# State reads with the token weights held in the array, in a fused attention and MoE kernel

## The chip, the cores and the metric

One core of one Trainium2 chip. The metric is the device time of one execution in microseconds (us), the median of several runs.

## The reference

Each of 8 batches has 8 heads; a head has 512 tokens (x) and 32 states, both 64 wide. Tokens read from states, states read from tokens, and both results, with the heads side by side, go through an MLP with a leaky activation.

```python
scores  = x @ state.T / 8                       # 512 x 32 for each batch and head
a       = softmax(scores, over the states);  xread = a @ state
scores2 = state @ x.T / 8                       # 32 x 512
a2      = softmax(scores2, over the tokens); sread = a2 @ x
rows    = concat([xread, sread]), heads side by side   # 8 * (512 + 32) rows of 512
h       = rows @ w_in                           # 512 x 2048
g       = max(h, 0) + alpha * min(h, 0)
out     = g @ w_out                             # 2048 x 512, float32
```

## The kernel before

The work is cut into small named steps, and one long string, ORDER, lists them in the order in which they are recorded; each engine runs its own steps in that order. So an order that was worked out ahead of time, not a loop, decides what stands behind what. A step is written as name.batch.further numbers; the last number of a step that writes PSUM is its bank.

The steps, by engine:

- GpSimd (POOL): `lx` loads a batch's x, `wi` and `wo` a quarter of w_in and w_out, `lst` the states, all by casting DMAs from float32 to float16; `ssh` subtracts the maximum of each state block, `snorm` divides by the sums, and `tn` (two for a batch, L413) multiplies the token weights by one over their sums.
- TensorE (PE): `xt` transposes x for the first two batches, `sc` computes scores (states as weights, 64x32 tiles), `m` multiplies the states of a head by their rows of w_in (64x32 tiles; h of a token is then its weights over the 8 x 32 states times this product, and xread itself is never computed), `f` and `F` compute h for one block of 128 hidden columns, `S` adds two such blocks to the output of 128 tokens, `L` does so in column pieces for the last tokens of batch 7, `rd` computes the state reads, and `F.8` with `R` takes the 256 state rows through the MLP. `Z` multiplies zeros, at the start alone.
- ScalarE (ACT): `sexp` and `te` (exponentials), `N` (the negative part of h), and most of the copies out of PSUM, `mo` and `O`.
- VectorE (DVE): `sb`, `smax`, `ssum`, `wb` (state softmax on transposed blocks), `tm` and `tsum` (maximum, and one over the sum, of the token softmax), `G` (the activation), and some of the copies.
- SyncE (SP): `xd` and `tt` are transposing DMAs, of x (batches 2 to 7) and of the token weights e2; `O` sends its output rows from here.

What the change touches: `state_reads` (L422) holds x (128 tokens x 64) as weights and streams 32 columns of the transposed token weights; the result has the layout that `XS` needs, so `rdo` only copies it. The token weights were divided by their sums before, by `tn`, ahead of `tt`. Heads 0 to 3 form half 0 and heads 4 to 7 half 1, and within a half the place of head h is `(h - 4 * g) ^ g`. PSUM has six single banks (`single`) and one pair (`two`), which scores use, and some of the m steps. The scores of batch 0 are computed in two halves and a third time as a whole. Tiles for m (7 batches), neg (4), gt and osb (4) come from rotating pools. `O` copies and stores in one step.

Of the kernel before, what the change touches and what calls it, by code (L numbers as in the profile page):

```python
# [8 lines left out]
F32 = mybir.dt.float32  # L9
F16 = mybir.dt.float16  # L10
# [19 lines left out]
G.0.8 G.0.11 N.0.10 S.0.2.3 mo.0.3.a.1 ssh.p.1 S.0.3.0.3 G.0.10 m.1.3 sexp.1 m.2.1.1.2 S.0.0.4  # L30
mo.2.1.a.1 S.0.2.4 mo.2.1.a.0 F.0.14.2 F.0.13.1 ssum.1 N.0.14 S.0.1.4 snorm.p.1 S.0.2.5 G.0.14
S.0.1.5 F.0.15.2 N.0.13 tsum.1 G.0.13 S.0.0.5 F.0.12.1 mo.1.3.a.1 N.0.15 S.0.3.1 S.0.3.2 wb.1 N.0.12
S.0.3.3 G.0.12 S.0.3.4 F.1.2.1 G.0.15 N.1.2 S.0.1.6 mo.1.3.a.0 tn.1.0 G.1.2 S.0.2.6 S.0.1.7 sc.2
tt.0 m.4.2.2.1 S.0.2.7 O.0.1.a F.1.3.0 mo.4.2.a.1 F.1.0.1 mo.4.2.a.0 F.1.1.2 O.0.2.a S.0.0.6 tm.2
N.1.3 N.1.1 S.0.3.5 F.1.5.4 sb.2 tn.1.1 N.1.0 S.0.0.7 G.1.3 lx.3 F.1.7.0 G.1.1 te.2.1 S.0.3.6 N.1.5
G.1.0 N.1.7 te.2.0 F.1.9.2 O.0.0.a G.1.5 N.1.9 S.0.3.7 G.1.7 O.0.3.a tsum.2 F.1.4.1 smax.2 N.1.4
F.1.6.4 S.1.2.0.0 F.1.8.5 G.1.9 tt.1 m.2.3 S.1.2.1 N.1.6 N.1.8 G.1.4 F.1.12.3 G.1.6 F.1.11.2 ssh.p.2
F.1.10.1 S.1.2.2 F.1.15.4 G.1.8 N.1.12 N.1.11 mo.2.3.a.0 S.1.1.0.5 S.1.1.1 N.1.10 S.1.2.3 G.1.12
G.1.11 G.1.10 sexp.2 xd.3 F.1.13.3 N.1.15 S.1.1.2 N.1.13 ssum.2 F.1.14.2 N.1.14 mo.2.3.a.1 S.1.1.3
G.1.13 G.1.14 S.1.2.4 S.1.1.4 S.1.1.5 G.1.15 m.3.2 mo.3.2.a.0 mo.3.2.a.1 m.3.1.1.3 rd.0.2 rd.1.4  # L40
sc.3 snorm.p.2 lx.4 rdo.0.a mo.3.1.v.0 wb.2 rdo.1.a m.2.2.1.2 mo.3.1.v.1 S.1.1.6 xd.4 S.1.2.5
S.1.2.6 F.2.4.4 S.1.1.7 F.2.2.3 mo.2.2.a.1 sb.3 S.1.2.7 S.1.0.0.2 tm.3 mo.2.2.a.0 N.2.4 F.2.15.1
O.1.1.a S.1.0.1 smax.3 S.1.0.2 F.2.0.5 O.1.2.v F.2.9.0 N.2.15 S.1.0.3 G.2.15 ssh.p.3 S.1.0.4 S.1.0.5
N.2.0 N.2.9 tn.2.1 sexp.3 S.1.3.0.1 G.2.0 F.2.13.5 G.2.4 G.2.9 S.1.0.6 te.3.1 ssum.3 N.2.2 N.2.13
G.2.13 F.2.12.4 F.2.8.0 N.2.12 N.2.8 S.1.3.1 S.1.3.2 G.2.12 S.1.3.3 te.3.0 G.2.2 F.2.1.5 S.1.0.7
F.2.5.4 N.2.1 F.2.3.3 G.2.8 S.1.3.4 snorm.p.3 F.2.11.0 tn.2.0 G.2.1 O.1.0.a N.2.5 S.1.3.5 N.2.11
tsum.3 S.1.3.6 N.2.3 G.2.5 m.3.3.2.5 sc.4 wb.3 F.2.6.4 tt.2 G.2.11 mo.3.3.a.1 mo.3.3.a.0 S.1.3.7
S.2.1.0.5 G.2.3 F.3.1.2 N.2.6 F.3.13.0 O.1.3.a F.2.10.3 N.3.1 G.2.6 tm.4 F.2.7.1 N.3.13 N.2.7 N.2.10
te.4.1 S.2.0.0.4 S.2.1.1 G.3.1 S.2.0.1 G.2.7 S.2.0.2 G.2.10 tn.3.1 F.2.14.2 F.3.2.1 N.2.14 S.2.1.2
S.2.1.3 sb.4 G.2.14 N.3.2 F.3.4.3 smax.4 S.2.1.4 S.2.1.5 lx.5 S.2.1.6 N.3.4 G.3.2 S.2.1.7 F.3.14.2  # L50
tn.3.0 O.2.1.a G.3.13 S.2.0.3 F.3.6.1 S.2.3.0.5 te.4.0 ssh.p.4 N.3.14 G.3.14 sexp.4 tsum.4 tn.4.1
N.3.6 G.3.4 S.2.0.4 F.3.8.0 tt.3 N.3.8 S.2.0.5 S.2.3.1 S.2.0.6 S.2.3.2 F.3.3.2 F.3.9.3 ssum.4
snorm.p.4 S.2.3.3 S.2.0.7 N.3.3 xd.5 S.2.3.4 G.3.8 N.3.9 G.3.3 S.2.3.5 m.6.0 G.3.6 G.3.9 m.5.1.0.2
rd.3.1 rd.2.3 O.2.0.a mo.6.0.v.1 mo.5.1.a.0 m.4.1.4.0 mo.5.1.a.1 mo.6.0.v.0 sc.5 rdo.3.a m.4.3.2.1
mo.4.1.a.1 S.2.3.6 F.3.11.0 rdo.2.a mo.4.3.a.0 wb.4 N.3.11 mo.4.1.a.0 S.2.2.0.3 F.3.0.2 mo.4.3.v.1
F.3.10.1 S.2.3.7 tm.5 S.2.2.1 S.2.2.2 G.3.11 N.3.0 F.4.1.4 sb.5 F.3.5.0 S.2.2.3 N.3.10 N.4.1 O.2.3.a
N.3.5 S.2.2.4 G.3.10 G.3.0 F.3.7.1 F.4.11.5 F.4.7.2 lx.6 G.4.1 N.4.11 N.3.7 S.2.2.5 S.2.2.6 smax.5
te.5.0 N.4.7 S.3.3.0.4 lx.7 S.2.2.7 G.3.5 ssh.p.5 S.3.3.1 O.2.2.a te.5.1 S.3.3.2 G.4.7 F.4.5.0
# [11 lines left out]
N.4.12 S.4.1.3 N.5.2 S.4.1.4 G.4.12 S.4.0.4 S.4.1.5 S.4.1.6 F.5.10.1 mo.7.0.a.1 S.4.0.5 ssh.p.6  # L70
G.5.1 sexp.6 G.5.2 F.5.0.5 F.5.5.0 N.5.0 S.4.1.7 S.4.0.6 N.5.10 S.4.0.7 G.5.12 G.5.0 tt.5 S.4.2.0.2
G.5.10 O.4.1.a N.5.5 rd.4.5 O.4.0.v rd.5.3 m.7.3.1.4 G.5.5 rdo.4.a m.6.2.5.0 rdo.5.a mo.6.2.a.0
ssum.6 sc.7 tsum.6 S.4.2.1 snorm.p.6 tn.6.0 S.4.3.0.3 mo.7.3.a.0 S.4.3.1 mo.7.3.v.1 S.4.2.2 F.5.11.5
S.4.3.2 sb.7 S.4.3.3 N.5.11 tn.6.1 G.5.11 F.5.6.1 F.5.9.4 S.4.2.3 S.4.2.4 F.5.7.5 S.4.3.4 mo.6.2.a.1
F.5.8.0 smax.7 S.4.3.5 S.4.3.6 wb.6 S.4.3.7 S.4.2.5 N.5.9 N.5.8 N.5.7 G.5.9 O.4.3.a G.5.8 F.5.4.4
# [12 lines left out]
N.8.2 N.7.2 S.6.2.1 G.8.2 S.6.2.2 N.7.6 S.6.1.7 F.7.14.4 G.7.6 F.7.10.0 G.7.2 S.6.2.3 N.8.9 N.7.14
# [16 lines left out]
def kernel(  # L105
# [51 lines left out]
    xgs = {}  # L157
# [494 lines left out]
```

## Time and profile before

| | |
|---|---|
| time, median of 3 runs | 217.57 us (217.44 to 217.98) |
| profiled execution, first to last instruction | 216.3 us (its own time is not listed apart from this) |
| PE busy | 208.6 us, 1637 matmuls |
| DVE / ACT / POOL busy | 164.8 / 137.6 / 71.1 us |
| HBM read and written | 17.31 and 8.91 MB |

A line of the profile's fifth part names the source line, the engine, the operation, what it writes and reads, shapes and the number of instructions, then busy time, mean nanoseconds of one, and the idle time in front of them with what ended it. In the timeline and in the chain, the first two numbers are the start and the length in us. Matmuls are pipelined: the length of a group holds the last one's way through the array, so the distance between the starts says what one costs.

### The profile page before, as it was taken

What the parts mean: (1) busy time and instruction counts of PE and PEld (TensorE: products, weight loads), DVE (VectorE), ACT (ScalarE), POOL (GpSimd) and SP (SyncE); (2) the same over time, 40 slices, a digit from 0 to 9 for tenths busy, and PEclk for the clock granted to TensorE, in tenths of its full rate; (3) what the DMA queues carried; (4) which work ended last, traced back from release to release, by engine and by line L of the source; (5) the groups of instructions that cost most, each with busy time, mean ns of one, the idle gap of its engine ahead of it and who ended that gap; (6) DMA issues with size and microseconds to landing.
All of it is one profiled execution on the core that took longest, in us unless ns stands there. A gap on an engine that the chain in (4) does not pass through costs nothing.

```text
span 216.3 us, 4190 instructions
## 1 busy us (share of the span) xinstructions
PE 208.6 (96%) x1637; PEld 99.3 (46%) x1637; DVE 164.8 (76%) x253; ACT 137.6 (64%) x271; POOL 71.1 (33%) x58
## 2 busy tenths in 40 slices
PE   7689999999999999999999999999999999999994
PEld 2433334444544444544444445444454455554553
DVE  3699988799999998999886869876798466665001
ACT  3399995998768957879449865566545346544021
POOL 7373858232367626314620112903500000000000
PEclk9999999999999999999999999999999999999999
DMA  6999999888475849596032532031430011110124
GB/s 82 165 202 203 205 187 184 107 240 141 47 129 167 109 88 194 100 192 149 18 83 97 134 63 100 2 97 50 52 147 27 25 48 48 48 48 4 48 100 145
DMA packets 39716, 23.12 MB, mean 107 GB/s; under 512 B 22144, under 2 KB 35984, under 8 KB 39696
## 3 DMA queue, kind: packets, MB, share of 16 engines
q0 software_dynamic: 12704, 8.62, 28.6%
q1 hardware_dynamic: 26960, 14.23, 25.4%
q8 instruction: 13, 0.21, 0.4%
q14 instruction: 7, 0.06, 0.1%
q10 hardware_dynamic: 32, 0.01, 0.0%
HBM read 17.31 MB, written 8.91 MB: 121 GB/s over the span
## 4 chain that ended last, share of the span: by engine, by line
PE 90%; DMA 5%; POOL 2%; issue 1%; ACT 0%; POOLq 0%
PE o L542 50%; PE h L490 25%; DMA w_in_sb<-in_moe_w_in_dram 5%; PE m_ps L457 4%; PE h L499 3%; PE o L590 3%; PE sr_ps L432 2%; PE o L562 2%; PE sc L307 1%; POOL xg L178 1%; POOL xg L161 0%; PE h L511 0%; POOL w_in_sb L197 0%; POOL st L191 0%; POOL ident masks.py:199 0%
## 5 line engine op out<-in xcount | busy, mean ns | idle before, releaser
L542 PE MATMUL o<-w_out_sb,gt 128*128 128x512 f16 x496 | 125.4, 379 | 0.0
L522 ACT ACTIVATE neg<-h 128x512 f32<-128x512 f32 (+1 forms) x144 | 77.6, 582 | 44.5 <-PE h L490 36.3
L530 DVE SCALAR_TENSOR_TENSOR gt<-neg,oma_sb,h 128x512 f16<-128x512 f32 x128 | 89.4, 737 | 18.7 <-ACT neg L522 18.3
L542 PEld LDWEIGHTS <-gt 128*128 128x128 f16 x496 | 47.5, 98 | 54.9 <-issue 2.9
L490 PE MATMUL h<-aT,m 128*128 128x512 f16 x250 | 68.7, 379 | 0.0
L490 PEld LDWEIGHTS <-m 128*128 128x128 f16 x250 | 24.1, 98 | 28.7 <-issue 0.9
L479 ACT CAST m<-m_ps 128x512 f16<-128x512 f32 x49 | 27.0, 603 | 6.4 <-PE m_ps L457 6.0
L413 POOL TENSOR_SCALAR e<-e,r 128x512 f16<-128x512 f16 x16 | 24.9, 1565 | 15.0 <-DVE r L409 13.8
L354 POOL TENSOR_TENSOR ts<-ts,mx 128x1024 f32<-128x1024 f32 (+1 forms) x9 | 15.5, 1719 | 42.2 <-DVE mx L348 42.2
L368 POOL TENSOR_TENSOR an<-ts,r 128x1024 f16<-128x1024 f32 (+1 forms) x9 | 15.4, 1720 | 25.2 <-DVE r L365 16.6
L580 ACT COPY osb<-o 128x512 f32<-128x512 f32 x23 | 13.7, 595 | 14.7 <-PE o L542 14.6
L457 PE MATMUL m_ps<-w_in_sb,stT 64*32 64x512 f16 x256 | 11.3, 383 | 0.5 <-DMA w_in_sb<-in_moe_w_in_dram 0.5
L399 ACT ACTIVATE e<-sc,nb 128x512 f16<-128x512 f32 x16 | 11.1, 704 | 0.4 <-DVE nb L391 0.4
L479 DVE CAST m<-m_ps 128x512 f16<-128x512 f32 x15 | 9.9, 677 | 1.4 <-PE m_ps L457 1.3
L530 DVE SCALAR_TENSOR_TENSOR gs<-neg,oma_sb,h 128x256 f16<-128x256 f32 x16 | 7.5, 476 | 4.5 <-ACT neg L522 4.5
L388 DVE TENSOR_REDUCE nb<-sc 128x2 f32<-128x1024 f32 x8 | 9.7, 1212 | 1.2 <-PE sc L307 1.2
L376 DVE STREAM_TRANSPOSE aT<-an 128x1024 f16<-128x1024 f16 (+1 forms) x9 | 10.0, 1115 | 0.7 <-POOL an L368 0.7
L364 DVE TENSOR_REDUCE r<-ts 128x32 f32<-128x1024 f32 (+1 forms) x9 | 9.8, 1089 | 0.7 <-ACT ts L360 0.7
L348 DVE TENSOR_REDUCE mx<-ts 128x32 f32<-128x1024 f32 (+1 forms) x9 | 9.8, 1090 | 0.0
L499 PE MATMUL h<-XS,w_in_sb 128*128 128x256 f16 x64 | 9.4, 273 | 0.0
L600 DVE COPY osr<-o 128x512 f32<-128x512 f32 x1 | 0.7, 692 | 11.3 <-PE o L590 11.3
L360 ACT ACTIVATE ts<-ts 128x1024 f32<-128x1024 f32 (+1 forms) x9 | 8.7, 971 | 0.0
(52 smaller groups left out, 117.6 us busy)
## 6 DMA issues: line engine op xcount, KB each, us to landing
out_dram<-osb SPq DMA_DIRECT2D x27, 256.0 KB, 2.4
xg<-in_x_dram POOLq DMA_DIRECT2D x7, 512.0 KB, 7.2
w_in_sb<-in_moe_w_in_dram POOLq DMA_DIRECT2D x4, 512.0 KB, 9.0
w_out_sb<-in_moe_w_out_dram POOLq DMA_DIRECT2D x4, 512.0 KB, 8.0
out_dram<-osb SPq DMA_DIRECT2D x9, 128.0 KB, 2.0
xg<-in_x_dram POOLq DMA_DIRECT2D x2, 256.0 KB, 4.9
out_dram<-osr SPq DMA_DIRECT2D x2, 256.0 KB, 2.5
st<-in_state_dram POOLq DMA_DIRECT2D x1, 224.0 KB, 5.6
```

The source lines that it names most:

```text
L354: engine(e).tensor_tensor(ts, ts, over_blocks(cols(live["mx", b], j, S // N)), ALU.subtract)
L368: engine(e).tensor_tensor(blocks(cols(live["an", b], j, S)), blocks(cols(live["ts", b], j, S)), over_blocks(cols(live["r1", b], j, S // N) ...
L399: nc.scalar.activation(live["e2", b][:, g, :, :], live["sc", b][:, :, :, g, :].rearrange("p r j s -> p (r j) s"), EXP, bias=live["nb", b][ ...
L413: nc.gpsimd.tensor_scalar_mul(e2, e2, live["r2", b][:, g : g + 1])
L457: nc.tensor.matmul(t[N * k : N * (k + 1), :], st_head(b, h)[64 * r : 64 * r + 64, :], w_in_sb[64 * r : 64 * r + 64, c, 512 * f : 512 * (f ...
L479: copier(e)(m_tile(b)[:, f, g, :], live["mp", b, f][g])
L490: nc.tensor.matmul(h.rearrange("p (r j s) -> p r j s", r=2, j=2), ms[b][:, f, g, 128 * j : 128 * (j + 1)], weights(b, g), start=(g == 0), ...
L499: nc.tensor.matmul(h, w_in_sb[:, c, 128 * jc : 128 * (jc + 1)], XS[:, c].rearrange("p q n b -> p (q n b)"), start=(c == 0), stop=(c == n_c ...
L522: nc.scalar.activation(neg, h, RELU, bias=0.0, scale=-1.0)
L530: nc.vector.scalar_tensor_tensor(gt, negs.pop((b, jc)), oma_sb[:, jc : jc + 1], h, ALU.mult, ALU.add)
L542: nc.tensor.matmul(outs[b, q], gts[b, jc][:, 128 * q : 128 * (q + 1)], w_out_sb[:, jc, :], start=(jc == 0), stop=(jc == n_jc - 1),)
L580: copier(e)(osb, t)
```

## The change

- `state_reads` swaps its operands: the transposed token weights of a head (128 tokens x 32 states) are the weights, on 128x32 tiles, and x is streamed, 64 columns. Four heads of a half run side by side; the result has states on partitions.
- `tn` is gone. The sums divide the small result: new step `rn` (VectorE, 128x128) multiplies by one over the sum and casts, new step `rt` transposes on TensorE, and `rdo` copies into `XS`.
- Heads of a half are every second one (g, g+2, ...), in loads, transposes, scores and m.
- One tile holds all eight PSUM banks, and every step names its banks; m, neg, gt and osb are fixed places, with the place as one more number of the step.
- `O` only copies; a new step `st` (`Ls` for the pieces) sends the rows, at a place of its own in the order. `S.8` takes the place of `R`.
- Batch 0's scores are computed once, in two halves.
- ORDER is new from end to end.

```diff
     def state_reads(b, bk):
         e2T = live.pop(("e2T", b))
-        t = live["sr", b] = single(bk, f"sr_ps{b}", [128, n_c, N], F32)
-        for c in range(n_c):
-            g = c // 2
+        t = live["sr", b] = single(bk, 2 * D).rearrange("p (g d) -> p g d", g=2)
+        for g in range(2):
             for q in range(n_q):
                 r, j = divmod(q, 2)
-                for i in range(2):
-                    h = 2 * c + i
-                    k = (h - 4 * g) ^ g
+                for k in range(4):
                     nc.tensor.matmul(
-                        t[D * i : D * (i + 1), c, :],
-                        xgs[b][:, h, j, r, :],
+                        t[N * k : N * (k + 1), g, :],
                         e2T[:, g, q, N * k : N * (k + 1)],
+                        xgs[b][:, 2 * k + g, j, r, :],
                         start=(q == 0), stop=(q == n_q - 1),
-                        tile_position=(0, D * i),
+                        tile_position=(0, N * k),
...
+    def state_reads_norm(b):
+        sn = live["sn", b] = att.tile([128, 2, D], F16, name=f"sn_{b}", tag="sn", bufs=2)
+        nc.vector.tensor_tensor(sn, live.pop(("sr", b)),
+            live["r2", b].unsqueeze(2).to_broadcast([128, 2, D]), ALU.mult)
+
+    def state_reads_transposed(b, bk):
+        t = live["srT", b] = single16(bk, 128)
+        nc.tensor.transpose(t, live.pop(("sn", b)).rearrange("p g d -> p (g d)"), ident)
...
-    def token_norm(b, g):
-        e2 = live["e2", b][:, g, :, :]
-        nc.gpsimd.tensor_scalar_mul(e2, e2, live["r2", b][:, g : g + 1])
...
-    def single(k, name, shape, dtype):
-        return ps.tile(shape, dtype, name=name, tag=f"k{k}", bufs=1)
-    def two(name, shape, dtype):
-        return ps.tile(shape, dtype, name=name, tag="two", bufs=1)
+    banks = ps.tile([128, 8, 512], F32, name="ps")
+    def single(k, w=512):
+        return banks[:, k, :w]
+    def two(k0, k1):
+        return banks[:, k0 : k1 + 1, :]
```

The new order where the prediction walks through it, from the loads to the first S steps, and at the end:

```
lx0.0 stc oma lx0.1 lst id wi.0 lx.1 wi.1 wi.2 Z.3.14 ... sc.0.0.6.7 ... wo.0 ssh.p.0.0 ... sc.0.1 ...
m.2.0.1.4 ... m.0.0.2.5 m.3.0.3.0 ... m.1.0.2.5 tt.0 ... wo.1 m.4.0.6.7 ... f.0.0.0.1 f.0.1.0.0 ... f.0.1.1
f.0.2.0.2 ... f.0.2.1 ... m.0.1.6.3 ... f.0.0.1 ... F.0.3.7 ... F.0.7.4 F.0.6.3 ... m.0.2.5.6 ... F.0.4.0 ...
F.0.5.2 ... m.1.1.1.6 ... F.0.10.5 ... F.0.9.4 ... S.0.0.0.7
...
S.8.0.7 L.7.3.0.2 O.8.0.a.2 L.7.3.0.3 L.7.3.0.4 L.7.3.0.5 st.8.0 L.7.3.0.6 L.7.3.0.7 LO.7.3.0.a Ls.7.3.0
```

The old order at the first of these places is `m.2.0 f.0.0.0.5 f.0.1.0.4 wi.2 ... f.0.1.1 ... m.0.1.1.3 f.0.0.1 ... m.1.1`, with `wo.0` ahead of `wi.2`, and it ends in `L.7.3.2.6 L.7.3.2.7 O.7.1.a LO.7.3.2.a`.

More of the change, by code (lines that the diff above doesn't have):

```diff
@@ L41 @@
[L41 to L46, printed above, removed]
@@ L70 @@
[L70 to L75, printed above, removed]
@@ L478, in state_w_in_out, with state_w_in @@
-    def state_w_in_out(b, f, e, g):
-        copier(e)(m_tile(b)[:, f, g, :], live["mp", b, f][g])
-    hs, negs, gts = {}, {}, {}
+    m_all = consts.tile([128, 26, 2, 512], F16)
+    def state_w_in(b, f, k0, k1):
+        live["mp", b, f] = (k0, k1)
+        for i in range(2):
+            for k in range(4):
+                g = (i + k) % 2
+                nc.tensor.matmul(
+                    banks[N * k : N * (k + 1), (k0, k1)[g], :],
+                    st_head(b, 2 * k + g)[64 * g : 64 * g + 64, :],
+                    w_in_sb[64 * g : 64 * g + 64, k, 512 * f : 512 * (f + 1)],
+                    start=True,
+                    stop=True,
+                    tile_position=(64 * g, N * k),
+                    skip_group_check=True,
+                )
@@ new lines, in state_w_in_out @@
+    def state_w_in_out(b, f, e, g, i=None):
+        if i is not None:
+            ms[b, f] = m_all[:, i]
+        copier(e)(ms[b, f][:, g, :], banks[:, live["mp", b, f][g], :])
+    hs, negs, gts = {}, {}, {}
+    neg_all = consts.tile([128, 4, 512], F32)
+    gt_all = consts.tile([128, 2, n_jc, S], F16)
+    gs_all = consts.tile([128, n_jc, B * N], F16)
+    for f in range(n_f):
+        for b in range(B):
+            gts[b, f] = gt_all[:, b % 2, 4 * f : 4 * (f + 1), :]
+        gts[B, f] = gs_all[:, 4 * f : 4 * (f + 1), :]
@@ L550, in token_rows @@
     def token_rows(b, q):
+        if b == B:
+            rows = out.rearrange("(b s) d -> b s d", s=S2)[4 * q : 4 * (q + 1), S:]
+            return rows.rearrange("b n d -> n b d")
         r, j = divmod(q, 2)
```

400 lines of the change are left out of this document (199 added, 201 removed).

## The prediction

> **What bounds the kernel now.** I read the page's busy shares first, then the chain that ended last, then the stages, and in the end single stretches of the timeline.
>
> ```profile
> PE 208.6 (96%) x1637; PEld 99.3 (46%) x1637; DVE 164.8 (76%) x253; ACT 137.6 (64%) x271; POOL 71.1 (33%) x58
> PE   7689999999999999999999999999999999999994
> PE 90%; DMA 5%; POOL 2%; issue 1%; ACT 0%; POOLq 0%
> ```
>
> TensorE is busy for 96% of the span and carries 90% of the chain; the rest of the chain is a start that waits for a DMA. The stages and the chain show where one gives way to the other:
>
> ```profile
> 10.80:16.20 5.40, 4.71 (x73) 2.14 (x72) 5.04 (x10) 5.40 (x13) 4.21 (x6) 1.00 1.35 202
> 16.20:21.60 5.40, 4.89 (x40) 1.82 (x41) 5.18 (x9) 5.12 (x11) 1.93 (x3) 1.00 1.22 203
> 43.00:65.00 22.00, 22.00 (x203) 10.16 (x202) 21.46 (x32) 17.99 (x37) 8.22 (x5) 1.00 0.75 140
> 173.00:195.00 22.00, 22.00 (x130) 12.49 (x128) 13.87 (x25) 11.30 (x27) 0.00 (x0) 1.00 0.13 48
> 5.69 11.84 DMA w_in_sb<-in_moe_w_in_dram
> 17.56 0.41 PE L457 MATMUL m_ps<-w_in_sb,stT 64*32 64x512 f16 x8 [0.51 <-DMA w_in_sb<-in_moe_w_in_dram]
> ```
>
> The columns after the stage's length are PE, PEld, DVE, ACT and POOL busy, the granted clock (1.00 throughout), DMA share and GB/s. The second quarter of w_in is issued at 5.69 and lands at 17.53; at 17.56 PE takes up step m.0.1, and from there to the last matmul no stage leaves it waiting: 22.00 of 22.00 in both late rows. So only three things count: the PE work left behind 17.56, what PE waits for in the new order, and the end. VectorE, at 21.46 of 22.00, is nearly full in the middle without holding PE.
>
> The profiled execution's own time is not listed beside its span of 216.3 us; I set the 1.27 us between span and median (217.57, three runs from 217.44 to 217.98) as what lies around it, and keep that unchanged.
>
> **The change part by part.** Prices of PE work come from these rows of the chain and of the timeline:
>
> ```profile
> 52.60 1.73 PE o L542 x8
> 54.33 0.56 PE m_ps L457 x16
> 54.88 1.12 PE sr_ps L432 x64
> 23.84 0.60 PE L542 MATMUL o<-w_out_sb,gt 128*128 128x512 f16 x2
> 24.38 0.41 PE L457 MATMUL m_ps<-w_in_sb,stT 64*32 64x512 f16 x8
> 24.72 0.60 PE L542 MATMUL o<-w_out_sb,gt 128*128 128x512 f16 x2
> 30.88 0.64 PE L457 MATMUL m_ps<-w_in_sb,stT 64*32 64x512 f16 x16
> 5.23 0.61 PE L287 MATMUL xT_ps<-ident,xg 128*128 128x128 f16 x8
> L287 PE MATMUL xT_ps<-ident,xg 128*128 128x128 f16 x32 | 2.5, 219 | 1.5 <-DMA xg<-in_x_dram 1.3
> 10.79 0.41 PE L307 MATMUL sc<-xT,stT 64*32 64x256 f16 x16
> ```
>
> A 512-column matmul takes 1.73/8 = 0.216. A second group of eight w_in matmuls adds 0.64 - 0.41 = 0.23, but a lone group costs 24.72 - (23.84 + 0.43) = 0.45: the change to small tiles and back costs about 0.2. A transpose takes its turn in (0.61 - 0.22)/7 = 0.056, with 0.22 as the length of one.
>
> *State reads.* Two batches take 1.12, less 0.1 for one change of tile shape: 0.51 for a batch, or, as two 64-column tiles run side by side, 16 rounds of 32 ns. The new form also has 32 matmuls, but four tiles side by side: eight rounds, each streaming 64 columns. At 0.216/512 a column that is 27 ns, so a round of 32 ns stays possible, 0.255 a batch, 8 x 0.25 = 2.0 saved. The bounds: 27 ns a round would save 2.35, and 16 ns for each matmul, as now, nothing. I take 32 ns: in the row of 16 w_in matmuls eight tiles do run at once, so four should.
> Against the change stands a rule of the Trainium skill, TensorE: Matmul & The Clock Gate, "Measured speedup vs the span model": weights load under a running matmul only when the row group differs, and all four new tiles span all rows. By that page's load time (columns over 1.2) a new round would be an estimated 27 + 27 = 54 ns, and the saving 0.6. The trace speaks against it: the same rule makes today's round 53 + 13, and it takes 32. Even if load and stream do alternate, today's row leaves 32 - 13 = 19 ns for 64 weight columns, so 9.5 + 27 = 37 ns in the new form and 0.3 us less saved, which lies within my range.
>
> *Transposes behind them (rt).* Eight at 0.056: +0.45. Their input comes from rn on VectorE, steps ahead of them in the order (rd.7 and rt.7 stand 1.5 us of matmuls apart, the least).
>
> *Order on PE.* Behind m.0.1 the old order changes to small tiles in 17 places, the new in 19: +0.4. Inside these, changes between reads and w_in or score matmuls fall from six to four: -0.2. Before m.0.1 the new order has five f matmuls and five m groups, the old three and four; PE waits there anyway, so 2 x 0.216 + 0.21 = 0.64 leaves the path. The third run of batch 0's scores (0.41) and a changed number of dummy matmuls lie ahead of 17.56 too: nothing. PE sum: -2.0 + 0.45 + 0.4 - 0.2 - 0.64 = -2.0.
>
> *Loads.* In the old order the transfers behind w_in's second quarter land one after the other:
>
> ```profile
> 12.53 0.78 POOL L203 DMA_DIRECT2D w_out_sb<-in_moe_w_out_dram  x1
> w_out_sb<-in_moe_w_out_dram POOLq DMA_DIRECT2D x1, 512.0 KB, 7.5
> 15.83 0.81 POOL L197 DMA_DIRECT2D w_in_sb<-in_moe_w_in_dram  x1
> w_in_sb<-in_moe_w_in_dram POOLq DMA_DIRECT2D x1, 512.0 KB, 6.8
> L479 ACT CAST m<-m_ps 128x512 f16<-128x512 f32 x49 | 27.0, 603 | 6.4 <-PE m_ps L457 6.0 <-DVE m L479 0.3
> ```
>
> That is 20.0 for w_out's first quarter and 22.6 for w_in's third, 2.5 apart at the 203 GB/s above. The new order swaps the two (wi.2, then wo.0), and issues both ahead of ssh, which costs POOL 1.6 us while it waits for VectorE anyway. From 17.6 on PE needs m.0.1, seven matmuls and two changes of shape to reach m.0.2, at 19.6; wi.2 lands at 20.0. Eight matmuls and two lone groups later it is at S.0.0.0 at 22.05, and wo.0 lands at 22.6. One wait carries the next, so together +0.55. ACT stands in the same place: m.0.1's copy has to pass before F.0.7, 0.6 us for which PE has only F.0.3 and half an f; within the 0.4 to m.0.2 that is hidden.
>
> *VectorE, ScalarE, GpSimd.*
>
> ```profile
> L413 POOL TENSOR_SCALAR e<-e,r 128x512 f16<-128x512 f16 x16 | 24.9, 1565 | 15.0 <-DVE r L409 13.8
> L409 DVE RECIPROCAL r<-r 128x2 f32<-128x2 f32 x8 | 1.2, 152 | 0.0
> L443 DVE CAST XS<-sr_ps 128x128 f16<-128x128 f32 x1 | 0.4, 444 | 0.2 <-PE sr_ps L432 0.2
> L580 DVE COPY osb<-o 128x512 f32<-128x512 f32 x8 | 5.5, 682 | 1.8 <-PE o L542 1.8
> L479 DVE CAST m<-m_ps 128x512 f16<-128x512 f32 x15 | 9.9, 677 | 1.4 <-PE m_ps L457 1.3
> ```
>
> GpSimd loses tn, 24.9 us; it is not on the path, so 0. On its queue lx.4 now waits for rd.0, with snorm.1, lx.3 and so wb.1 behind it; but rd.0 stands ahead of smax.1, which ssh.1 before lx.4 needs in any case, so 0 (were rd.0 late, batch 1's weights would be late by as much). VectorE gets eight rn (never seen; between a 128x2 reciprocal's 0.15 and this row's 0.44, I take 0.44): 3.6; three more O and one more rdo: 2.5; two m copies fewer: -1.4. That makes 169.5 of 215, and by the new order's counts no stretch of PE work is fuller than today's 43 to 65. +0.1 for small waits, 0 to 2 as bounds.
>
> *Stores.* Copy and store are two steps now, on the same four buffers; SP has nothing PE waits for but through them. The end:
>
> ```profile
> 213.35 0.27 ACT L573 COPY osb<-o 128x128 f32<-128x128 f32 x1 [0.26 <-PE o L562]
> out_dram<-osb SPq DMA_DIRECT2D x9, 128.0 KB, 2.0
> out_dram<-osb SPq DMA_DIRECT2D x2, 64.0 KB, 1.8
> ```
>
> The last piece is 256 columns wide instead of 128: copy +0.1, store +0.2, so +0.3.
>
> Sum: -2.0 + 0.55 + 0.1 + 0.3 = -1.05. The span goes from 216.3 to 215.3, the time to about 216.6. With the reads' bounds and the wait for loads from 0 to 0.9, this case's own range is 215.8 to 217.2.
>
> **The rivals.** First, the loads come later. Step tt.0, which had to wait for tn, now follows the exponentials directly, and falls at about 16 to 20 us, into saturated rings:
>
> ```profile
> e2T<-e SPq DMA_TRANSPOSE x8, 3.3
> ```
>
> The last column is us to landing. Its input, 128x1024 in two bytes, is 256 KB; at 203 GB/s that is 1.26 us that the loads lose. Each load behind it lands 1.2 later, S.0.0.0 waits 1.75 instead of 0.55: 217.8. For it: the DMA rows are full at that time; against it: no row shows a transposing DMA beside a load, and it may yield to them.
>
> Second, slower: the reads gain nothing, since 16 ns for each matmul is a limit of issuing and not of rounds. Then PE's sum is 0 instead of -2.0: 218.6. The point at which this decides: a round of 32 + 1.0/64 = 48 ns makes the change worth nothing. For it: no row shows four 128x32 tiles. Against it: the 16 w_in matmuls above follow each other at 0.23 for eight and are limited by their 512 columns alone.
>
> Third, the new order leaves gaps in the middle: VectorE has 0.54 us to spare in 43 to 65, and rn, the O copies and their waits for a store's buffer fall somewhere. One microsecond in two such stages gives 218.6. For it: all places are new; against it: the shortest ways from an F to the S that needs it, 2.0 to 2.6 us of PE work, are about as long as today's 2.2 to 2.6, and PE didn't wait with these.
>
> That the change does not do what it says I rule out: the built program has the eight transposes and no tn.
>
> **How the numbers follow.** Forecast 0.47, loads later 0.21, reads without gain 0.12, gaps 0.15, something else 0.05 on both sides. 0.3%, about 0.65 us, is what a measurement of this kernel can tell from no change: faster is below 216.92. Of the forecast 0.40 lies there, and 0.04 of the others: 0.44. Within it: 0.07 of the forecast, 0.15 of the late loads, 0.02 of the gaps: 0.24. Slower: 0.04 + 0.12 + 0.13 + 0.03 = 0.32. The range of 215.5 to 218.9 takes in the forecast's own and all three rivals.
>
> **What would show it.** Right: two batches' reads in about 0.6 us instead of 1.12; m.0.2 and S.0.0.0 with waits for a DMA of about half a microsecond together; PE at 22.00 of 22.00 in the middle; the last matmul about 3.3 before the end. Wrong: reads of still 0.5 a batch; a wait of over 1.5 before S.0.0.0; any PE wait for VectorE or ScalarE behind 40 us.

## The result, and the profile after

The changed kernel takes 230.94 us (median of 4 runs, 228.94 to 232.36) against 217.66 us (4 runs, 217.44 to 217.98): a ratio of 1.058, interval 1.052 to 1.065. Executions of one kernel fall into a faster and a slower state; medians and ranges here take in all, ratios and their intervals the faster ones alone, and the profiled executions of e5 and e8 are slower ones. The prediction said 216.6, with a range from 215.5 to 218.9. It was wrong in sign and far outside its range.

The profiled execution took 228.94 us, the lowest of the four, with a span of 227.2 us: 10.9 more than before. Lines of its page first: busy times, the slices of PE and of the granted clock, and the chain by engine.

```profile
PE 211.4 (93%) x1630; PEld 98.3 (43%) x1630; DVE 167.6 (74%) x261; ACT 137.2 (60%) x271; POOL 46.1 (20%) x42
PE   5969799299998999999999999999999999999993
PEclk9999999769999999999999999999999999999999
PE 79%; DMA 10%; DVE 3%; POOL 2%; ACT 2%; issue 1%; ACTq 0%; POOLq 0%
```

The loss has a place. The eighth slice, 39.8 to 45.4 us, has a PE of 2 tenths, and there and in the slice behind it the clock falls to 7 and 6 tenths; behind 51 us the row is full again. DMA's share of the chain went from 5 to 10%. The same by stages (stage and length, then PE, PEld, DVE, ACT and POOL busy, clock, DMA share, GB/s):

```profile
21.60:24.30 2.70, 2.70 (x19) 1.04 (x20) 2.70 (x5) 2.70 (x7) 0.00 (x0) 1.00 1.41 124
...
27.00:32.40 5.40, 4.44 (x64) 1.89 (x63) 4.40 (x8) 3.65 (x9) 1.83 (x1) 1.00 1.36 203
32.40:43.00 10.60, 6.80 (x44) 2.78 (x40) 6.86 (x10) 5.23 (x10) 3.76 (x4) 0.98 1.31 177
43.00:65.00 22.00, 21.22 (x157) 8.65 (x157) 16.62 (x24) 15.44 (x31) 3.58 (x2) 0.85 0.57 73
```

From 32.4 to 43 PE stands for 3.8 us while the DMA engines are full, and in the stage behind it it is "busy" for 21.2 of 22 us at a clock of 0.85: busy time that does less work. What it waits for is in the chain, and in the waits of PE (in all, times, longest):

```profile
16.69 11.23 DMA w_out_sb<-in_moe_w_out_dram
27.96 2.75 PE ps L565 x12
30.71 0.35 PE ps L442 x32
...
33.05 10.70 DMA xT<-xg
43.78 0.63 PE ps L320 x16
```

```profile
PE ps L320 <- DMA xT<-xg: 4.6, 1, 4.6
...
PE ps L510 <- ACT e L416: 1.3, 2, 0.7
PE ps L565 <- DMA w_out_sb<-in_moe_w_out_dram: 1.2, 1, 1.2
```

PE reaches the scores of batch 2 (sc.2, L320) at 39.2 and stands until x of batch 2 has come through its transposing DMA (xd.2). The issues in the windows around that time (last column: us to landing), first of the kernel before, then of the changed one:

```profile
xT<-xg SPq DMA_TRANSPOSE x1, 4.5
```

```profile
e2T<-e SPq DMA_TRANSPOSE x1, 11.3
...
xg<-in_x_dram POOLq DMA_DIRECT2D x1, 512.0 KB, 10.3
xT<-xg SPq DMA_TRANSPOSE x1, 10.7
```

xd.2 was issued 0.9 us earlier than before (33.05 against 33.94), and took 10.7 us in place of 4.5. POOL's and SP's rows of the timeline show its company, before and after:

```profile
26.19 0.94 POOL L161 DMA_DIRECT2D xg<-in_x_dram  x1
27.13 0.76 POOL L203 DMA_DIRECT2D w_out_sb<-in_moe_w_out_dram  x1
...
33.94 3.12 SPq L274 DMA_TRANSPOSE xT<-xg  x1
...
38.47 0.97 POOL L161 DMA_DIRECT2D xg<-in_x_dram  x1
```

```profile
18.23 0.91 POOL L175 DMA_DIRECT2D xg<-in_x_dram  x1
19.10 1.52 POOL L217 DMA_DIRECT2D w_out_sb<-in_moe_w_out_dram  x2
...
32.43 0.93 POOL L175 DMA_DIRECT2D xg<-in_x_dram  x1
33.05 5.22 SPq L285 DMA_TRANSPOSE xT<-xg  x1
...
44.35 2.74 PE L565 MATMUL ps<-w_out_sb,gt_all 128*128 128x512 f16 x6
```

Before, the next load of x was issued when xd.2 had landed (33.94 + 4.5 = 38.4). Now one (lx.4) goes out 0.6 us ahead of it. The first rows show a second change of company: the load of batch 2's x (lx.2, 26.19 before, 18.23 now) had one quarter of w_out behind it and now has two. Before, that quarter landed at 36.4, 2.5 us behind the start of xd.2; now the two land at 35.5 and 38.5, 2.4 and 5.4 behind it. The last row is the second half of the loss: six matmuls that start 0.43 us apart, where the chain before had 0.216; twelve run so, from 44.35 to 49.4.

The account, from the starts of the matmuls: the waits and slow matmuls of the changed kernel behind 19 us, against 0.14 us before, and the rest.

| | us |
|---|---|
| PE reaches m.0.1 at 18.58, not 17.56 | +1.0 |
| F.0.7 waits for m.0.1's copy (19.4) | +0.6 |
| S waits for w_out's second quarter (26.4) | +1.4 |
| sc.2 waits for xd.2 (38.8) | +4.6 |
| twelve matmuls at half clock behind it | +2.5 |
| F waits for a bank of the scores (70.2 and 91.5) | +1.6 |
| PE's work itself | -2.05 |
| last matmul to the end, 4.1 instead of 3.2 | +0.9 |
| sum (the span grew by 10.9) | +10.6 |

### The profile page after: what moved, and what is told of

It is laid out like the page before. It is cut to its first block, busy times and chain, and to the rows that moved or that the text cites. A ratio compares the mean times of both kernels' runs of the same rounds, so it can differ in the third digit from the quotient of the medians.

```text
span 227.2 us, 4141 instructions
## 1 busy us (share of the span) xinstructions
PE 211.4 (93%) x1630; PEld 98.3 (43%) x1630; DVE 167.6 (74%) x261; ACT 137.2 (60%) x271; POOL 46.1 (20%) x42
## 4 chain that ended last, share of the span: by engine, by line
PE 79%; DMA 10%; DVE 3%; POOL 2%; ACT 2%; issue 1%; ACTq 0%; POOLq 0%
PE ps L565 46%; PE ps L510 21%; DMA w_out_sb<-in_moe_w_out_dram 5%; DMA xT<-xg 5%; PE ps L519 3%; PE ps L479 3%; PE ps L230 2%; PE ps L587 2%; PE ps L442 1%; PE ps L320 1%; DVE ts L357 1%; ACT e L416 1%; POOL an L387 1%; POOL xg L192 1%; ACT neg_all L542 1%
## 5 line engine op out<-in xcount | busy, mean ns | idle before, releaser
L565 PE MATMUL ps<-w_out_sb,gt_all 128*128 128x512 f16 x496 | 125.2, 383 | 1.2 <-DMA w_out_sb<-in_moe_w_out_dram 1.2
L542 ACT ACTIVATE neg_all<-ps 128x512 f32<-128x512 f32 (+1 forms) x144 | 76.9, 583 | 44.9 <-PE ps L510 31.8
L546 DVE SCALAR_TENSOR_TENSOR gt_all<-neg_all,oma_sb,ps 128x512 f16<-128x512 f32 x128 | 89.5, 739 | 15.3 <-ACT neg_all L542 14.3
L565 PEld LDWEIGHTS <-gt_all 128*128 128x128 f16 x496 | 47.6, 99 | 57.5 <-issue 6.4
L510 PE MATMUL ps<-aT,m_all 128*128 128x512 f16 x250 | 68.0, 383 | 1.7 <-ACT e L416 1.3
L510 PEld LDWEIGHTS <-m_all 128*128 128x128 f16 x250 | 24.0, 99 | 32.4 <-issue 5.1
L492 ACT CAST m_all<-ps 128x512 f16<-128x512 f32 x51 | 27.8, 599 | 9.5 <-PE ps L479 9.5
L609 ACT COPY osb_all<-ps 128x512 f32<-128x512 f32 x22 | 12.9, 598 | 15.9 <-PE ps L565 15.9
L416 ACT ACTIVATE e<-ps,nb 128x512 f16<-128x512 f32 x16 | 11.0, 691 | 3.8 <-DVE ts L357 3.8
L479 PE MATMUL ps<-w_in_sb,stT 64*32 64x512 f16 x256 | 11.4, 382 | 1.4 <-ACT stT L275 0.7
L357 DVE STREAM_TRANSPOSE ts<-ps 128x1024 f32<-128x1024 f32 x7 | 8.7, 1246 | 5.3 <-PE ps L320 4.5
L395 DVE STREAM_TRANSPOSE aT<-an 128x1024 f16<-128x1024 f16 (+1 forms) x9 | 10.1, 1117 | 1.3 <-POOL an L387 1.3
## 6 DMA issues: line engine op xcount, KB each, us to landing
w_in_sb<-in_moe_w_in_dram POOLq DMA_DIRECT2D x4, 512.0 KB, 11.7
```

The costliest lines, as they stand in the source:

```text
L357: nc.vector.transpose(softmax_tile("ts", b).rearrange("p (r s) -> p r s", r=2), sc.rearrange("p g r t -> p r (g t)"),)
L416: nc.scalar.activation(live["e2", b][:, g, :, :].rearrange("p (r j) s -> p r (j s)", r=2), live["sc", b][:, g], EXP, bias=live["nb", b][:, ...
L479: nc.tensor.matmul(banks[N * k : N * (k + 1), (k0, k1)[g], :], st_head(b, 2 * k + g)[64 * g : 64 * g + 64, :], w_in_sb[64 * g : 64 * g + 6 ...
L492: copier(e)(ms[b, f][:, g, :], banks[:, live["mp", b, f][g], :])
L510: nc.tensor.matmul(h.rearrange("p (r t) -> p r t", r=2), ms[b, f][:, g, 128 * j : 128 * (j + 1)], weights(b, g), start=(g == 0), stop=(g = ...
L542: nc.scalar.activation(neg, h, RELU, bias=0.0, scale=-1.0)
```

## The experiments

Theory A: the transposing DMAs and loads that now lie beside each other hold each other up, PE waits, and then runs at half clock. Theory B: the new order's waits on VectorE and ScalarE. Theory C: the head runs at half clock because PE is idle early. Theory D: loads are late because they are issued late. Each ratio is against the kernel before, run beside it (medians from 217.8 to 218.1). A change of order is given as the place of one step.

### e1: lx.4 behind lx.3

```diff
-... S.0.2.3 lx.4 sexp.1 ... S.0.1.5 lx.3 wb.1 ...
+... S.0.2.3 sexp.1 ... S.0.1.5 lx.3 lx.4 wb.1 ...
```

> The changed kernel with one step moved: lx.4, the load of batch 4's x, is issued behind lx.3 instead of 6 us ahead of it, so that it is not in the DMA rings while xd.2, the transposing DMA of batch 2's x, runs. Theory A (the rings: xd.2 takes 10.7 us instead of 4.5 because w_out's last quarters and lx.4 share the rings with it; PE waits 4.6 us in front of sc.2 and then runs 12 matmuls at half clock): xd.2 lands by about 39.5 instead of 43.7, the wait falls under 1 us, the half clock is gone; about 6.5 us less, 224.5. Theory B (the new order leaves gaps wherever VectorE and ScalarE come late, and sc.2 is only the first): the gap moves to the next steps, at most 2 us less, 229.

Measured: 224.8 us (223.3 to 227.8), ratio 1.030 (1.022 to 1.036).

```profile
PE ps L320 <- DMA xT<-xg: 2.1, 1, 2.1
```

One load moved brings 6 us: xd.2, issued at 33.05 as before the move, lands in 7.7 us in place of 10.7. The wait did not fall below 1 us as A had it; part of the half clock (8 matmuls) is still there. What still lies beside xd.2 are the two quarters of w_out: the next load of x is issued 5 us behind its start. It is 6.6 or more behind in e7 and e15 below, where xd.2 takes 7.7 and 8.3 us; in the old order, with one quarter, it takes 4.5. So about half of what xd.2 lost goes with that change of order; no run moves these quarters alone, so this part isn't shown apart.

### e2: zeros while PE waits

```diff
+Z.2.84
 sc.2.2.2.3
```

> The changed kernel with 21 dummy matmuls of zeros (512 columns, 4.5 us) in front of sc.2, where PE waits 4.6 us for xd.2. The transfer and the wait are as they were; only PE is not idle in it. Theory A: what follows the wait runs at full clock, 12 matmuls at 0.216 instead of 0.427, 2.5 us less, 228.4. Theory B (those 12 matmuls are slow because of their operands' transfers, or the time is lost later anyway): no change.

Measured: 229.87 (229.6 to 230.7), ratio 1.056 (1.054 to 1.058).

```profile
43.00:65.00 22.00, 22.00 (x174) 9.48 (x172) 16.08 (x24) 15.50 (x32) 3.01 (x2) 1.00 0.52 85
...
PE ps L565 <- DMA w_out_sb<-in_moe_w_out_dram: 2.8, 1, 2.8
```

The clock behind the wait for xd.2 is 1.00 in place of 0.85: kept busy, PE has no slow stretch there. The time fell by 1.1 and not by A's 2.5, since in this execution the wait for w_out grew from 1.2 to 2.8, half clock came behind that one, and xd.2 started 1.9 us later: the landing times differ from run to run. The stretch behind the wait for w_out:

```profile
29.40:33.00 3.60, 3.26 (x8) 1.13 (x8) 1.32 (x3) 1.95 (x6) 2.19 (x2) 0.53 1.37 201
```

### e3: more zeros at the head

```diff
-Z.3.14 stt.2
+Z.3.24 stt.2
```

> The changed kernel with its first dummy matmuls lengthened from 14 to 24 units, as the kernel before has them, so that PE is busy until the identity is there at 4.1 us instead of idle from 2.8. Theory C (the first 9.5 us run at half clock because of that idle time, and this delays batch 0's softmax and step m.0.1, at 18.6 instead of 17.6): full clock from about 5 us, m.0.1 0.9 us earlier. By theory A this is mostly swallowed by the wait for xd.2, which depends on the loads alone: 0 to 0.5 us less in the end; by theory B all of it comes through, 0.9 less.

Measured: 230.08 (229.7 to 231.3), ratio 1.058 (1.054 to 1.061). m.0.1 came 0.75 us earlier, so C holds for the head. With it there, m.0.2 and S.0.0.0 waited 0.24 and 0.68 us for their DMAs, where in the changed kernel, late as it was, they waited nothing; and the wait before sc.2 grew from 4.6 to 5.7. The head isn't what sets the time while loads do.

### e4: without tt.0

```diff
-m.1.0.2.5 tt.0 ... wo.3
+m.1.0.2.5 ... wo.3 tz.0        # memset on POOL
```

> The changed kernel without tt.0, the transposing DMA of batch 0's token weights at 16 us; a memset on GpSimd writes zeros in its place, so batch 0's state reads are left out of the output. Theory A: the loads from w_out's second quarter on land 2 to 2.5 us earlier (25.5 instead of 27.9, x of batch 2 at 30.5 instead of 33.0), the 1.4 us wait for w_out shrinks to about 0.2, xd.2 starts 2.5 us earlier and has fewer loads beside it from then on; 3 to 5 us less, 226 to 228. Theory D (the loads yield nothing to it, they are late because GpSimd issues them late): no change in the landings, at most 0.5 us less.

Measured: 223.2 (222.8 to 224.2), ratio 1.025 (1.023 to 1.028).

```profile
30.04 5.04 SPq L285 DMA_TRANSPOSE xT<-xg  x1
...
PE ps L320 <- DMA xT<-xg: 1.5, 1, 1.5
```

Without tt.0 w_out's second quarter lands at 24.7 in place of 27.9, which D had ruled out, and xd.2 starts 3.0 us earlier. It still takes 10.1 us (lx.4 goes out 2.3 behind its start), so it lands 3.6 earlier, at 40.2 in place of 43.7. The wait for w_out is gone, sc.2 waits 1.5 and no matmul runs at half clock: 7.7 us, more than A had expected, because the half clock goes with the wait. The two waits and the half clock give 1.4 + 3.1 + 2.5 = 7.0 of it.

### e5 and e8: the new reads in the old order, and tt.0 early in it

e5 is the kernel before, its own order and places, with heads by stride two, the new reads (two batches in one bank), and no tn. e8 moves tt.0 in it to where the exponentials end.

```diff
 # e5
-rd.0.2 rd.1.4 sc.3 ... rdo.0.a mo.3.1.v.0 wb.2 rdo.1.a m.2.2.1.2 ...
+rd2.0.1.4 sc.3 ... mo.3.1.v.0 rn.0 rn.1 wb.2 m.2.2.1.2 rt2.0.1.4 rdo.0.a rdo.1.a ...
-tn.*  (16 steps)
 # e8, on top
+te.0.1 te.0.0 tt.0 mo.1.0.v.1 wo.0
```

> The kernel before, with its own order and places, and of the change only the heads by stride two, the m matmuls interleaved over both banks, and the new reads: stationary token weights on 128x32 tiles, two batches to one bank, then the division by the sums on VectorE (rn), one transpose a batch (rt) and the copies (rdo); the eight divisions' sixteen POOL steps (tn) are gone. If the prediction's first step was right (reads -2.0 us, transposes +0.45) and the order alone is what costs: 216.0 us, ratio 0.990 to 0.995. If the new reads bring a cost of their own (PE waiting for the division, or the bank): 217.6 us or more, with a PE wait before the rt line.

> The same as e5, but the transposing DMA of batch 0's token weights (tt.0) issued as soon as its exponentials are done, among the weight loads, as the new order does. Theory A (a transposing DMA among the loads takes about 11 us in place of 1.3 to 3 and sets the loads behind it back): w_out's second quarter, w_in's last and x of batch 2 land 1 to 3 us later than in e5 and the time is 1 to 3 us above e5. If the transposing DMA costs the loads nothing: within 0.3 us of e5.

Measured: e5 223.32 (220.1 to 223.9), ratio 1.017 (1.013 to 1.021); e8 225.63 (223.1 to 226.7), ratio 1.033 (1.029 to 1.037). e5: POOL's and SP's rows, issues, and waits.

```profile
32.32 3.34 SPq L274 DMA_TRANSPOSE xT<-xg  x1
...
34.64 0.95 POOL L161 DMA_DIRECT2D xg<-in_x_dram  x1
```

```profile
xT<-xg SPq DMA_TRANSPOSE x1, 8.7
```

```profile
PE sc L307 <- DMA xT<-xg: 2.4, 1, 2.4
...
PE sc L307 <- DVE m L486: 0.9, 1, 0.9
PE o L549 <- ACT XS L452: 0.5, 1, 0.5
```

This was not expected. The order of the loads is the old one, but POOL, without the 1.57 us steps of tn in its queue, is through with them earlier: lx.3 goes out at 34.64 in place of 38.47, and so beside xd.2, which takes 8.7 us. The wait of 2.4 us is followed by seven matmuls at half clock. That isn't all of the loss: executions of e5 with a mean clock of 0.998 to 1.00 still took 220.1 to 223.1 us. e8 adds 2.3 us by the medians, within A's 1 to 3, and 3.5 by the ratios, above it; one of its stages, its chain and its first wait show why.

```profile
20.00:23.00 3.00, 2.38 (x17) 0.90 (x17) 3.00 (x7) 2.76 (x6) 0.00 (x0) 1.00 1.71 60
```

```profile
14.66 11.69 DMA w_in_sb<-in_moe_w_in_dram
...
PE m_ps L475 <- DMA w_in_sb<-in_moe_w_in_dram: 5.0, 2, 4.0
```

While tt.0 runs among the loads, the DMA engines are busier (1.71) and move less (60 GB/s where the loads alone had 203 to 206): w_in's third quarter needs 11.7 us, where e5 has 7.2, PE waits 4.0 us for it, and half clock follows.

### e6, e7 and e15: the changed kernel, its loads taken apart

e6 has all the work of the changed kernel, with tt.0 behind tt.1, batch 0's reads beside batch 1's in the other half of their bank, and lx.4 behind them. e7 adds e3's zeros and a last piece 128 wide. e15 adds an S step ahead of each of three matmuls that wait for a bank.

```diff
 # e6
-tt.0 wo.1 ... rd.0.5 ... lx.4 ... tt.1 ... rd.1.7
+wo.1 ... tt.1 tt.0 ... rd.1.7 rd.0.7.256 lx.4
 # e15, on top of e7
-m.0.3.6.4 S.0.0.3 ... F.2.9.0 ... S.1.0.3 ... F.3.10.0 ... S.2.2.3
+S.0.0.3 m.0.3.6.4 ... S.1.0.3 F.2.9.0 ... S.2.2.3 F.3.10.0
```

> The changed kernel with all its work, but tt.0 issued behind tt.1, batch 0's reads done beside batch 1's in the other half of their bank, and the load of x of batch 4 (which needs batch 0's x buffer) behind them: what e1 and e4 tried singly, without leaving work out. Theory A: xd.2 starts near 30 us and lands before sc.2 needs it, PE has no half clock in 38 to 50 us, 221.5 to 222.5 us. Theory B (the new order's waits on VectorE and ScalarE are what costs): 228 us or more.

> e6 with two more mends: 24 in place of 14 blocks of dummy matmuls ahead of the first transposes, so that the head runs at full clock (e3 gave 0.75 us at the head, then swallowed by the loads), and the last piece of the last tile 128 wide in place of 256. Theory A with C: the 0.75 us now shows, and 0.3 to 0.5 at the end: 220.3 to 221.3. If loads still bound the start: the same as e6 less 0.4.

> e7 with three S steps moved ahead of the matmuls that wait for banks of the scores: S.0.0.3 ahead of m.0.3 (waited 1.04 us), S.1.0.3 ahead of F.2.9 (0.83), S.2.2.3 ahead of F.3.10 (0.71). Theory B in small (te waits for sb on VectorE and frees the banks late): each wait falls by 0.4, 1.2 us in all, 220.2 to 220.8. If the S steps are missed later, where they filled other waits: as e7, 221.6.

Measured: e6 223.2 (221.6 to 223.3), ratio 1.023 (1.021 to 1.026); e7 221.63 (221.1 to 223.9), ratio 1.020 (1.016 to 1.023); e15 221.1 (220.3 to 222.0), ratio 1.013 (1.010 to 1.016). In e6 no wait before sc.2 and no slow matmul is left: xd.2 takes 8.9 us there, but starts at 29.8. It came out 0.7 us above A's range, and its profiled execution has 5.7 us from the last matmul to the end, where the changed kernel had 4.1. e7's profiled execution is 2.0 us shorter than e6's: the head's 0.75, less 0.6 that sc.2 then waits again, brings the last matmul only 0.4 earlier, and the other 1.6 is e6's longer end. e7 came out 0.3 us above its range. The piece of 128 brought nothing: from the last matmul to the end it is 4.1 us. What still waits in e7, by the waits of PE and the timeline:

```profile
PE ps L510 <- ACT e L416: 1.2, 2, 0.7
...
PE ps L479 <- ACT e L416: 0.9, 1, 0.9
```

```profile
26.46 1.24 DVE L357 STREAM_TRANSPOSE ts<-ps 128x1024 f32<-128x1024 f32 x1
...
27.74 0.69 ACT L416 ACTIVATE e<-ps,nb 128x512 f16<-128x512 f32 x1 [1.39 <-DVE ts L357]
```

te (L416) starts only when sb (L357) has read the same two banks, and PE gets them back when te is done. In e15 each of the three waits fell by 0.43 us, from 1.04 to 0.61, from 0.83 to 0.40 and from 0.71 to 0.28, as expected, but others came behind them (0.61 at 29.8, 0.41 at 65.0, 0.19 twice). The time fell by 0.5 us by the medians, by 1.5 by the ratios, whose intervals meet; whether the 1.2 expected came isn't settled. So B holds in small: what is left in the new order lies for a good part in waits of this kind and in the end, and moving single steps shifts them.

### e9 to e12: is it POOL's queue, or the reads?

e9 is e5 with the division left on POOL: all tn at their old places, rn a plain copy. e10 is the kernel before, with lx.3 moved. e11 mends two waits in e9 (rn.3 and rn.2 behind the copy that sc.5 needs, and S.4.2.2 ahead of S.4.3.0). e12 is e5 with these mends and lx.3 behind ssh.2.

```diff
 # e9, against e5
+tn.*  (16 steps, old places)
-nc.vector.tensor_tensor(sn, sr, r2 (broadcast), ALU.mult)
+nc.vector.tensor_copy(sn, sr)
 # e10, against the kernel before
-snorm.p.1 ... tn.1.0 ... tn.1.1 ... lx.3
+snorm.p.1 lx.3 ... tn.1.0 ... tn.1.1
```

> e5 with the division left where the kernel before has it: the sixteen POOL steps (tn) stand at their old places in POOL's queue, and rn is a plain copy. In e5 POOL, without tn, issued the load of x of batch 3 at 34.64 us in place of 38.47, beside the transposing DMA xd.2, which took 8.7 us in place of 4.5; PE waited 2.4 us and then ran some 5 us at half clock. Theory P (the POOL steps held the loads apart, and their removal is what e5 lost): no wait before sc.2, full clock in 43 to 54 us, 217.0 to 217.8 us (reads -1.6, the waits of 0.93, 0.52 and 0.29 at the three other pairs stay). Theory Q (the new reads themselves cost): 221 us or more.

> The kernel before with one token of its order moved: the load of x of batch 3 (lx.3) directly behind snorm.1 on POOL, so that it is issued near 35.4 us in place of 38.47, while xd.2 (from 33.94) runs. Nothing else is changed. Theory P: xd.2 takes 7 to 9 us in place of 4.5, PE waits about 2 us before sc.2 and runs behind it at half clock: 220 to 222.5 us. Theory Q: as before, 217.8 us.

> e9 with two waits of its own taken out: rn.3 and rn.2 behind the m copy that sc.5 waits for (0.93 us), and one more S step ahead of the matmul that waits for the bank of pair 4, 5 (0.52 us). Theory P: 215.8 to 216.6 us, faster than the kernel before, and so the first step of the prediction (reads) right by itself. Theory Q: 219.5 us or more.

> e5 (division on VectorE, no POOL steps) with the same two mends, and the load of x of batch 3 issued behind ssh.2 on POOL, some 10 us later and so apart from xd.2. Theory P: no wait before sc.2, no half clock, 215.8 to 216.8 us. If the load then comes too late for xd.3: a wait before sc.3, 217 to 218. Theory Q: 220 us or more.

Measured: e9 220.14 (219.4 to 220.5), ratio 1.009 (1.007 to 1.011); e10 221.2 (219.6 to 227.0), ratio 1.013 (1.008 to 1.018); e11 218.58 (218.3 to 220.0), ratio 1.003 (1.001 to 1.005); e12 225.54 (224.7 to 227.6), ratio 1.036 (1.031 to 1.040). xd.2's landing in e9, then e10's, and the waits of PE in e10 and e12:

```profile
xT<-xg SPq DMA_TRANSPOSE x1, 4.5
```

```profile
xT<-xg SPq DMA_TRANSPOSE x1, 7.2
```

```profile
PE sc L307 <- DMA xT<-xg: 2.1, 1, 2.1
```

```profile
PE sc L307 <- DMA xT<-xg: 5.7, 1, 5.7
```

Theory P, of the expectations: tn's steps in POOL's queue kept lx.3 off xd.2. With tn back there xd.2 takes 4.5 us again and sc.2 doesn't wait. And in the kernel before, where nothing else is changed, one load issued at 35.23 makes xd.2 7.2 us long and PE wait 2.1. That is P, shown from both sides. P's half clock did not come in e10's profiled execution (behind the wait the matmuls start 0.216 us apart); three others have a mean clock of 0.968 to 0.992 and took 222.2 to 227.0 us. e12 is the closest pair to e5: w_out's last quarter lands at 35.3 and 35.4, only lx.3 goes out elsewhere, and xd.2 takes 4.5 us in place of 8.7. Its sc.2 doesn't wait either, but the load is now too late for xd.3, and sc.3 waits 5.7: the second case of its expectation, larger than put there.

But e9 and e11 missed P's numbers by 2.3 and 2.0 us: with the loads as before, the new reads still bring no gain.

### e13 and e14: where the reads' gain goes

Against e11 each pair of reads is copied (rn) and copied out (rdo) in one instruction each; the copy rn on ScalarE (e13) or on VectorE (e14).

```diff
-rn.0 rn.1 ... rdo.0.a rdo.1.a
+rn2.0.1.a ... rdo2.0.1.a       # e14: rn2.0.1.v
```

> e11, but each pair of reads is copied in one instruction of 256 elements a partition on ScalarE in place of two on VectorE, and copied out behind its transposes in one in place of two. Theory V (VectorE's queue gives the reads' gain back): the waits of e11 at 60.9, 87.8 and 89.5 us (0.30, 0.21, 0.13) go and 0.6 to 1.2 us with them: 217.2 to 218.0. If ScalarE is as late as VectorE: 218.6 or more.

> As e13, but the one copy stays on VectorE. Theory V: between e11 and e13, 217.8 to 218.4. If the place of the copy doesn't matter: as e13.

Measured: e13 218.51 (217.5 to 221.4), ratio 1.0006 (0.998 to 1.003); e14 218.79 (218.1 to 219.9), ratio 1.0035 (1.001 to 1.006). In e11 the wait at the first pair reads, in the timeline:

```profile
61.53 0.59 PE L500 MATMUL h<-aT,m 128*128 128x512 f16 x2 [0.25 <-DVE osb L590]
```

An output copy on VectorE, late by the rn copies ahead of it, holds a bank that F needs. In e13 this wait (0.30) is gone, in e14 it is 0.23. So V, by which the copy rn on VectorE delays that bank, is right about this wait. What it is worth isn't clear of noise: e13 is 0.1 us below e11 by the medians, 0.3% by ratios whose intervals overlap. e13 is level with the kernel before; V's 217.2 to 218.0 was missed by 0.5, and e14, forecast between e11 and e13, came out level with e11. Against the kernel before, the matmuls of e11 fall back by 0.41, 0.61 and 0.27 us around the first three pairs and gain 0.39 at the last, though each pair's reads are 0.4 us shorter; at the second pair there are four short stops, 0.87 us in all, of which the trace names one, for a copy of m on VectorE (0.15); the rest isn't settled. No version beat the kernel before.

## Why the prediction was wrong

**The step that failed is "Loads", and with it the sentence on the engines "GpSimd loses tn, 24.9 us; it is not on the path, so 0".** The walk of the loads ended at S.0.0.0, at w_out's first quarter. Behind it stood two more landings that PE needs: w_out's second quarter (1.4 us) and x of batch 2 through xd.2 (4.6 us, and 2.5 us of half clock behind it). xd.2 was never costed: its 4.5 us were taken along silently as a constant. It is none: here it took 10.7. That a load of x beside it lengthens it is shown (e1, e5, e10, e12); that the second quarter of w_out, now behind lx.2, has a part in it is likely, not shown apart. And POOL is not only arithmetic: its queue issues every load, so its busy steps are also what sets the loads apart. In the old order, taking tn away moved a load earlier onto a transposing DMA that is on the path (e5 against e9: 3.2 us by the medians, 1.8 by the ratios). In the changed kernel the runs show lx.4's place (e1), tt.0's (e4) and both (e6); none puts tn back there.

**"lx.4 now waits for rd.0 ... so 0" failed in the same way.** The question asked was what waits behind lx.4; the one that mattered was what it runs beside. That one load cost 6 us, the half clock with it (e1).

**The first rival was the right mechanism, far too cheap.** It had tt.0 among the loads and took 1.26 us of bandwidth for it, priced at S.0.0.0. Measured, w_out's second quarter comes 3.2 us later by it and x of batch 2 3.6 later (e4), and the time is 7.7 us longer, because a wait of that length also costs clock. The remark that no row shows a transposing DMA beside a load was the warning: the term had no upper bound, and the range gave it none. tt.0 and lx.4 aren't additive: either one away removes more than half of the wait.

**"The dummy matmuls lie ahead of 17.56: nothing" failed by 1.0 us.** The head runs at half clock in the new order and m.0.1 comes 1.0 later (e3 gives back 0.75 of it). The head's transposes of x start 0.106 us apart, in the kernel before 0.056. As long as the loads come later still, that delay is hidden behind them. The first rows of "Loads" were near in size all the same: with the head at full speed m.0.2 and S.0.0.0 wait 0.9 us together (e3), against 0.55 forecast (0.4 by the prices given there, as 19.6 and eight matmuls at 0.216 and two groups at 0.45 come to 22.2 and not 22.05); that the changed kernel shows none of it is luck, as PE came late. And F.0.7 waited 0.6 for m.0.1's copy, which was forecast hidden.

**Reads: right.** The starts of the matmuls give 7.9 ns each, eight rounds of 32 ns, 0.25 a batch, as forecast; the row with `L442 x32` in the chain has 0.35 with the change of shape, where two batches took 1.12. PE's work fell by 2.05, forecast -2.0. The weight-load rule that spoke against it (the Trainium skill, "TensorE: Matmul & The Clock Gate", as the prediction cites it) would have given an estimated 54 ns a round; the 32 ns measured disagree with it. (That page has the rule under "The mechanism" and the load time under "LDWEIGHTS (loading the stationary operand)", not under the heading that the prediction names.) What failed is the last sentence of the sum: that work taken off PE comes off the time. In the old order with the old loads (e11) it doesn't. Its trace places a part of the difference in waits for VectorE and ScalarE (0.25, 0.15 and 0.27 us); the rest has no place. This is the second rival's outcome, as far as placed by the third rival's cause.

**Middle, VectorE and ScalarE: +0.1 forecast, +1.6 measured,** within the bounds of 0 to 2. The place was not seen: te waits for sb, and a bank of the scores comes back late. The rn took 0.28 us each, not 0.44:

```profile
L454 DVE TENSOR_TENSOR sn<-ps,r 128x128 f16<-128x128 f32 x8 | 2.3, 284 | 1.7 <-PE ps L442 1.7
```

**End: +0.3 forecast, +0.9 measured.** e7 shows that the width of the last piece isn't the reason. The last output rows land 2.6 us after the last matmul in place of 2.3, as forecast, and what follows them to the end takes 1.5 in place of 0.9; why isn't settled.

**The signs named ahead.** The reads were as short as said, and S.0.0.0 did not wait over 1.5 us. The other signs of "right" failed: m.0.2 and S.0.0.0 did not wait for DMAs, PE was at 21.2 of 22.0 in the middle, and the last matmul came 4.1 us before the end. Of the signs of "wrong" the last one came, PE waits for ScalarE at 70.2 and 91.5 us; yet the largest wait, before 44 us, was for a DMA, which no sign named.

## What to carry to other kernels

Before work is taken off an engine that also issues DMAs, write down at what time each of its DMAs goes out with and without that work, and what each will then run beside: an idle engine's queue may be the spacing that the transfers need. Walk the loads to the last landing that the critical engine needs, not to the first, and treat the duration of a transfer on the path as a quantity that its neighbours set. And a wait on TensorE of a few microseconds is to be priced with the slow matmuls behind it.

## What the runs showed of the hardware

- A transposing DMA beside loads is slow and slows them. xd.2 (the same transfer each time) took 4.5 us with one quarter of w_out landing 2.5 us behind its start and the next load of x issued after it (before, e9), 7.2, 7.7 and 8.7 with a load of x issued 1.1, 2.1 and 2.3 us behind its start (e10, e8, e5), 7.7 with two quarters of w_out and no load of x until 5 us behind its start (e1), and 10.7 and 12.6 with these quarters and a load of x 0.6 us ahead of or behind its start (after, e3). tt.0 took 3.1 us in the kernel before and 11.3 among loads (after, e8); in e8 the DMA engines' busy share was 1.71 meanwhile and the rate fell to 60 GB/s. "DMA: Bandwidth & Descriptors" of the Trainium skill, "Rules for kernel authors", says that a transpose next to ordinary DMAs needs nothing; for correct data that may be so, for the time these runs say otherwise.
- The clock halves after short waits, and not always. After waits of 4.6 us (after) and 5.7 us (e12) some 5 and 3.4 us of matmuls ran at half clock, 0.43 us apart; after 4.0 us (e8), 2.8 (e2), 2.4 (e5) and 2.1 (e1) some 3 us did so, after 2.1 us in e10 and 1.5 us in e4 none. The stretches at half clock in the records are 6.8 us long (42.66 to 49.48, after) or 3.4 us (42.24 to 45.65, e1). "TensorE: Matmul & The Clock Gate" of the Trainium skill, Part 1, has the window free-running and about 3.4 us long: the lengths of these stretches agree with it, and the free start agrees with waits of 2.1 us that once cost clock and once didn't; the length as a lower limit of the wait does not, as 2.1 us can be enough.
